# A decode step of two layers: W2 loaded twice, its buffer lent to a head's keys, the lead matrix dropped

## The chip, the cores and the metric

The kernel runs on one core of a Trainium2 chip. A core has a matrix engine (TensorE, PE in the profile; PEld is its weight load), a vector engine (VectorE, DVE), a scalar engine (ScalarE, ACT), GpSimd (POOL) and SyncE (SP, which here only issues transfers), and 16 transfer (DMA) engines that move data between the chip's main memory (HBM) and the on-chip buffer SBUF. Matrix products land in banks of a second small memory, PSUM. The metric is the device time of one execution in microseconds; lower is better.

## The reference

One token passes through attention with a cache, a dense block, and both once more with the same weights and the same cache. All data are float32.

```python
def _A_ref(x, k_cache, v_cache, wq, wo):            # H=32 heads, Sk=8192, Dh=128, D=640
    q = (x @ wq).reshape(1, 1, 32, 128).transpose(0, 2, 1, 3)
    scores = einsum("bhqd,bhkd->bhqk", q, k_cache) * 128 ** -0.5
    o = einsum("bhqk,bhkd->bhqd", softmax(scores), v_cache)
    return o.transpose(0, 2, 1, 3).reshape(1, 1, 4096) @ wo
def _B_ref(x, w1, w2):                              # Dff=1728
    return maximum(x @ w1, 0) @ w2
for _ in range(2):
    x = x + _A_ref(layernorm(x), k_cache, v_cache, wq, wo)
    x = x + _B_ref(layernorm(x), w1, w2)
```

Keys and values of a head are 4 MB each, so all 32 heads hold 268 MB. Both layers read all of them, and little of it fits on chip.

## The kernel before, in words

**The stream.** Keys and values come through one large buffer, `ring` (L94). Its room is counted in units of 8 numbers per partition, which over 128 partitions are 4 KB; `RING` is 3496. `UNITS` (L41 to L54) says in which pieces each head's cache is loaded: as a rule one load of all keys (1024 units, 4 MB) and one of all values; the heads at the ends of the layers are cut finer. `pump` (L123) issues, on SP's queue and in order, as many loads of the list `todo` as find room; `place` (L110) looks for the smallest free gap that holds the load in one piece. Each time PE has used a piece, `release` (L158) frees it and calls `pump` again. In SP's program the load stands behind a wait for the product that used the room last.

**Two layers, back and forth.** Layer 1 takes the heads 0 to 31, layer 2 the heads 31 to 0. What the ring holds at the end of layer 1 is not loaded again: head 31 whole and head 30 but for its first four units (`kept`, L96; together exactly `RING`). Those four (600 units) go to other buffers that are no longer needed then: `load_beside` (L143) loads them into `wqc`, `mix`, `lead` and `wct` as each is free. After that the ring takes head 29's keys when the first scores of layer 2 release room.

**One head.** `scores` (L361) multiplies the query with the keys, `exponentials` and `rows_weighed` do the softmax, `turn` transposes the weights, `values` (L420) multiplies with the values, `output` (L439) combines four rows. The heads' outputs are multiplied with `wo` in fours.

**The end of a layer.** The product of the last head's output with its `wo` rows and then W1 is not made one after the other: during the layer `mixing` and `mixing_quarter` (L474, L501) form the product of that part of `wo` with W1 in `mix`, so that `mlp` (L772) gets the hidden row from `o` with `mix` directly (L775). The hidden row is turned into columns `hT` (L822 to L859), passed through the ReLU, and multiplied with W2 in 14 blocks of 128 rows (`w2_t`, L877 to L901). Blocks 0 to 3 are summed on DVE into `by_rows` (L837, L887) and go through PE as one; the others go one by one.

**The start of layer 2.** The query of head 31, with which layer 2 begins, needs the layer norm of the whole output of layer 1. To have it sooner, layer 1 keeps the weights of that head's query in `wqc`, centred (`centred_weights`, L516), and forms the product of W2 with them in `lead` (`leading`, L532, one block in each of the heads 15 to 28) and that of the last head's output weights in `wct` (`leading_of_output`, L569). In `mlp` the query then follows from the hidden columns and `lead` (`lead_of`, L810), and the first scores of layer 2 begin while the output products of layer 1 still run (the `yield`s at L896 and L910). The scale from the layer norm follows later, in the exponentials (L380).

**Work beside the stream.** `due` (L669) puts side work in two lists; `work_off` does a step of it between the pieces of a head. W1, W2 and `wqc` are loaded on ACT's queue at the heads 4, 7 and 9 of layer 1 (L683 to L689), `wq` and `wo` in groups of four heads on the same queue.

Of the kernel before, what the change touches and what calls it, by code (L numbers as in the profile page):

```python
# [75 lines left out]
FB = 4 * F_TILES + F_REST  # L76


@with_exitstack
def decode_kernel(ctx: ExitStack, tc: tile.TileContext, x, kv, wq, wo, w1, w2, out):  # L80
# [41 lines left out]

    def pump():  # L123
        while todo:
# [3 lines left out]
            at = place(layer, n)  # L128
# [45 lines left out]
    def load_wq(g, queue):  # L174
        t = wts.tile([P, NB * HG * DH], F32, name="wq_t")
        n = NB * DH * (HG if g < NG - 1 else HG - 1)
        wq_t[g] = t[:, :n].rearrange("p (c n) -> p c n", c=NB)
        queue.dma_start(t[:, :n], wq[P * g : P * g + P, :n])
# [36 lines left out]


    wqc = consts.tile([P, NB, DH], F32, name="wqc")
    lead = consts.tile([P, FB, DH], F32, name="lead")

# [77 lines left out]
    second = []  # L297

    def weights_of(g, c, j):

        if g == NG - 1 and j == HG - 1:
            if not second:
                return wqc[:, c]
            j = 0
        return wq_t[g][:, c, j * DH : (j + 1) * DH]

    def queries(g, xc, r):

        pq = ps_m.tile([P, 512], F32, name="px")
        for c in range(NB):  # L310
            for j in range(HG):
# [3 lines left out]
                    weights_of(g, c, j),  # L315
# [200 lines left out]
    def centred_weights():  # L516
        pt = ps_m.tile([P, 512], F32, name="px")
        for c in range(NB):
            nc.tensor.matmul(
                pt[:, :DH],  # L520
                ones.to_broadcast([P, P]),
                wqc[:, c],
                start=(c == 0),
                stop=(c == NB - 1),
            )
        yield "dve"
        for c in range(NB):
            nc.vector.scalar_tensor_tensor(  # L528
                wqc[:, c], pt[:, :DH], -1.0 / D, wqc[:, c], op0=ALU.mult, op1=ALU.add
            )  # L530

    def leading(b):  # L532

        if b % 4 == 0:
            pt = ps_m.tile([P, 512], F32, name="px")
            n = min(4, FB - b)
            for i in range(n):
                for g in range(4):
                    nc.tensor.matmul(
                        pt[32 * g : 32 * g + 32, i * P : (i + 1) * P],  # L540
                        w2_t[:, b + i, g * DR + P : (g + 1) * DR],
                        ident,
                        start=True,
                        stop=True,
                    )
            yield "dve"
            nc.scalar.copy(lead[:, b : b + n].rearrange("p b d -> p (b d)"), pt[:, : n * P])
            yield "pe"
        pt = ps_m.tile([P, 512], F32, name="px")
        for c in range(4):  # L550
            nc.tensor.transpose(
                pt[:, c * P : (c + 1) * P], w2_t[:, b, c * DR : c * DR + P], ident
            )
        yield "dve"
        nc.scalar.copy(wct[:, :4].rearrange("p c d -> p (c d)"), pt)
        yield "pe"
        pt = ps_m.tile([P, 512], F32, name="px")
        for c in range(NB):
            nc.tensor.matmul(  # L559
                pt[:, :DH],  # L560
                wct[:, c] if c < 4 else lead[:, b],
                wqc[:, c],
                start=(c == 0),
                stop=(c == NB - 1),
            )
        yield "dve"
        nc.scalar.copy(lead[:, b], pt[:, :DH])

    def leading_of_output():  # L569

        pt = ps_m.tile([P, 512], F32, name="px")
        for c in range(NB):
            nc.tensor.matmul(
                pt[:, :DH], wct[:, c], wqc[:, c], start=(c == 0), stop=(c == NB - 1)
            )
        yield "dve"
        nc.scalar.copy(wct[:, 4], pt[:, :DH])

# [12 lines left out]
    def attention_and_mlp(L, xr, s, before=None):  # L591
# [44 lines left out]
        def before_last():  # L636
# [13 lines left out]
            if L == 0:  # L650
                pq = ps_m.tile([P, 512], F32, name="px")
                mlp_in.append(pq)
                for c in range(NB):
                    g = c % 4
                    nc.tensor.matmul(
                        pq[32 * g : 32 * g + 32, :DH],
                        xpc[:, c : c + 1].to_broadcast([P, 32]),
                        wqc[:, c],
                        start=c < 4,
                        stop=c in (2, 3, 4),  # L660
                        skip_group_check=True,
                    )
                load_beside(0, wqc.rearrange("p c d -> p (c d)"), NB * DH)
# [5 lines left out]
        def due(h):  # L669
# [20 lines left out]
            if L == 0 and where == MIX_AT[0][-1]:  # L690
                slow.append([centred_weights(), "pe"])
# [6 lines left out]
            if L == 0 and where == MIX_AT[L][-1] + 1:  # L698
                slow.append([leading_of_output(), "pe"])
            if where in LEAD_AT[L]:  # L700
                slow.append([leading(LEAD_AT[L].index(where)), "pe"])

# [69 lines left out]
    def mlp(L, o, last, xp, ph, pq=None):  # L772
# [7 lines left out]
        if L == 0:  # L780
            nc.tensor.matmul(
                pq[32:64, :DH],
                o.to_broadcast([P, 32]),
                wct[:, 4],
                start=False,
                stop=True,
                skip_group_check=True,
            )
        else:
            in_wait(64)  # L790
# [15 lines left out]
        if L == 0:  # L806
            nc.scalar.copy(xp[:, :DH], pq[:, :DH])
            pl = ps_m.tile([P, 512], F32, name="px")

        def lead_of(blocks):  # L810
            for b in blocks if L == 0 else ():
# [29 lines left out]
        if L:  # L841
            first_row()
# [164 lines left out]
```

## Time and profile before

| | us |
|---|---|
| median of 3 runs | 1367.67 (1367.07 to 1367.99) |
| the profiled execution, its own time | 1367.95 |
| its span, first to last instruction | 1366.1 |
| PE busy in it | 1000.2 (73%) |
| DVE, ACT busy | 182.7, 113.2 |

The profile divides the span into 40 slices of 34 us and gives for each the busy share of the engines in tenths, the granted PE clock, the share of the 16 DMA engines and what they moved. Further views list transfers by size, the chain of waits that ended last, the instructions in order of time, and busy times in chosen stretches. A tile is named without its buffer number; `w_t` stands for both W1 and W2, `in_kv` is the cache in HBM.

### The profile page before, as it was taken

To read this page: it belongs to the slowest core of one execution; us is meant where nothing else is said; L and a number is where in the kernel's file an instruction comes from. 1 tells how busy PE (TensorE), PEld (TensorE's weight loads), DVE (VectorE), ACT (ScalarE), POOL (GpSimd) and SP (SyncE) were. 2 spreads that over 40 slices of the span, in tenths; PEclk is the share of its full clock that TensorE was granted. 3 is DMA by queue.
4 is the path that set the end of the run, shared out by engine and by line. 5 is a ranking of instruction groups with operands and counts; after the bars stand their busy time and mean duration, and the time that the engine had idled before them with its cause. 6 is when DMAs were issued, how large, how long until landed. Compare 5 with 4: busy or idle time off the path is not lost.

```text
span 1366.1 us, 16729 instructions
## 1 busy us (share of the span) xinstructions
PE 1000.2 (73%) x7546; PEld 408.1 (30%) x7546; DVE 182.7 (13%) x696; ACT 113.2 (8%) x305; POOL 2.9 (0%) x10
## 2 busy tenths in 40 slices
PE   6674757778777777687798867677777677677768
PEld 2221312322333333333344322232223222222224
DVE  1010100111101111111122111110111111111112
ACT  0000000100101101111001000000001000000000
POOL 0000000000000000000000000000000000000000
PEclk8676777987888988987799777787779788887788
DMA  9999999999999999999979999999999999999994
GB/s 396 432 431 427 435 428 429 430 432 431 428 428 434 428 432 430 427 429 423 424 295 415 436 430 428 429 430 429 435 430 430 429 429 433 429 432 431 428 426 192
DMA packets 29023, 572.70 MB, mean 419 GB/s; under 512 B 3220, under 2 KB 3352, under 8 KB 5656
## 3 DMA queue, kind: packets, MB, share of 16 engines
q1 hardware_dynamic: 24056, 525.19, 89.9%
q10 hardware_dynamic: 4896, 46.45, 8.1%
q8 instruction: 59, 0.97, 0.3%
q14 instruction: 12, 0.10, 0.0%
HBM read 571.62 MB, written 0.00 MB: 418 GB/s over the span
## 4 chain that ended last, share of the span: by engine, by line
DMA 67%; PE 29%; DVE 2%; ACT 1%; issue 1%; SPq 0%; POOLq 0%; POOL 0%; ACTq 0%; DVEq 0%
DMA ring<-in_kv 65%; PE outs L427 10%; PE ps L366 10%; PE px L506 2%; PE pt L393 1%; DMA wo_t<-in_wo 1%; DMA wq_t<-in_wq 1%; PE px L312 1%; ACT p L385 1%; PE acc L332 1%; PE acc L582 1%; DVE h_t L378 1%; PE pm L413 1%; PE pm L453 0%; PE px L559 0%
## 5 line engine op out<-in xcount | busy, mean ns | idle before, releaser
L366 PE MATMUL ps<-ring,spread_q 128*32 128x512 f32 (+2 forms) x2064 | 315.9, 726 | 174.1 <-DMA ring<-in_kv 173.6
L427 PE MATMUL outs<-ring,pT 128*4 128x512 f32 (+2 forms) x2128 | 330.0, 770 | 57.1 <-DMA ring<-in_kv 56.9
L366 PEld LDWEIGHTS ps<-ring,spread_q 128*32 128x32 f32 x2064 | 61.0, 126 | 287.2 <-DMA ring<-in_kv 183.7
L427 PEld LDWEIGHTS outs<-ring,pT 128*4 128x4 f32 x2128 | 57.0, 101 | 264.2 <-issue 192.4
L378 DVE TENSOR_REDUCE h_t<-ps 128x1 f32<-128x512 f32 x64 | 44.2, 691 | 464.6 <-PE ps L366 464.4
L453 PE MATMUL pm<-h_t,p 128*128 128x1 f32 (+1 forms) x512 | 69.6, 258 | 33.1 <-DVE p L444 33.1
L453 PEld LDWEIGHTS pm<-h_t,p 128*128 128x128 f32 x512 | 64.4, 194 | 95.0 <-DVE p L444 93.4
L385 ACT ACTIVATE p<-ps,h_t 128x512 f32<-128x512 f32 x63 | 43.3, 687 | 556.9 <-DVE h_t L378 542.9
L393 PE MATMUL pt<-row_of,p 128*128 128x16 f32 x512 | 68.9, 267 | 22.8 <-ACT p L385 22.6
L444 DVE COPY p<-outs 128x256 f32<-128x256 f32 x62 | 26.3, 425 | 357.4 <-PE outs L427 357.4
L393 PEld LDWEIGHTS pt<-row_of,p 128*128 128x128 f32 x512 | 62.8, 193 | 34.6 <-ACT p L385 34.4
L445 ACT COPY p<-outs 128x256 f32<-128x256 f32 x62 | 23.1, 372 | 462.6 <-DVE p L444 462.6
L406 PE MATMUL pm<-ident,h_t 128*128 128x128 f32 x128 | 31.1, 325 | 40.2 <-DVE h_t L378 40.2
L506 PE MATMUL px<-w_t,wct 128*128 128x448 f32 (+1 forms) x80 | 46.7, 671 | 0.2 <-DVE wqc L528 0.2
L406 PEld LDWEIGHTS pm<-ident,h_t 128*128 128x128 f32 x128 | 19.0, 187 | 90.8 <-DVE h_t L378 88.7
L413 PE MATMUL pm<-h_t 128*128 128x1 f32 x128 | 26.9, 280 | 24.5 <-DVE h_t L410 24.5
L312 PE MATMUL px<-wq_t,ln_xc 128*32 128x128 f32 x630 | 30.8, 362 | 0.0
L312 PEld LDWEIGHTS px<-wq_t,ln_xc 128*32 128x32 f32 x630 | 26.3, 150 | 15.0 <-issue 14.0
L413 PEld LDWEIGHTS pm<-h_t 128*128 128x128 f32 x128 | 21.5, 210 | 30.8 <-DVE h_t L410 30.8
L332 PE MATMUL acc<-wo_t,o_cols 128*32 128x160 f32 x496 | 28.4, 384 | 0.0
L332 PEld LDWEIGHTS acc<-wo_t,o_cols 128*32 128x32 f32 x496 | 20.9, 145 | 19.4 <-issue 15.5
L506 PEld LDWEIGHTS px<-w_t,wct 128*128 128x128 f32 x80 | 13.7, 216 | 38.0 <-issue 36.9
(151 smaller groups left out, 343.2 us busy)
## 6 DMA issues: line engine op xcount, KB each, us to landing
ring<-in_kv SPq DMA_DIRECT2D x104, 4096.0 KB, 25.3
ring<-in_kv SPq DMA_DIRECT2D x27, 2048.0 KB, 23.8
ring<-in_kv SPq DMA_DIRECT2D x19, 1024.0 KB, 20.0
wo_t<-in_wo ACTq DMA_DIRECT2D x14, 1280.0 KB, 17.4
wq_t<-in_wq ACTq DMA_DIRECT2D x13, 1280.0 KB, 17.2
w_t<-in_w ACTq DMA_DIRECT2D x1, 4480.0 KB, 25.6
w_t<-in_w ACTq DMA_DIRECT2D x1, 4320.0 KB, 24.5
ring<-in_kv SPq DMA_DIRECT2D x3, 768.0 KB, 27.6
```

The costliest lines, as they stand in the source:

```text
L312: nc.tensor.matmul(pq[32 * j : 32 * j + 32, :DH], xc[:, c : c + 1].to_broadcast([P, 32]), weights_of(g, c, j), start=(c == 0), stop=(c == ...
L332: nc.tensor.matmul(acc[32 * g : 32 * g + 32, :DR], col.to_broadcast([col.shape[0], 32]), wt[:, g * DR : (g + 1) * DR], start=first, stop=last,
L366: nc.tensor.matmul(hd.ps[32 * g : 32 * g + 32, c : c + n], spread_q[:, 3 - r : 35 - r], tile_of[:, at + g * n : at + (g + 1) * n], start=f ...
L378: nc.vector.tensor_reduce(hd.nm, hd.ps, AX.X, ALU.max, negate=True)
L385: nc.scalar.activation(hd.p, hd.ps, AF.Exp, bias=hd.nm, scale=scale, accum_out=hd.l)
L393: nc.tensor.matmul(pt[:, 16 * b : 16 * b + 16], hd.p[:, b * P : (b + 1) * P], row_of.rearrange("p g r -> p (g r)"), start=True, stop=True,)
L406: nc.tensor.matmul(pt[:, :P], hd.nm.to_broadcast([P, P]), ident, start=True, stop=True)
L413: nc.tensor.matmul(pt[:, :1], hd.l.to_broadcast([P, P]), hd.wi, start=True, stop=True)
L427: nc.tensor.matmul((hd.out if r0 < 3 else hd.out_3)[32 * g : 32 * g + 4, r0:r1].rearrange("p r d -> p (r d)"), hd.pT[:, 4 * i : 4 * i + 4] ...
L444: nc.vector.tensor_copy(oc[:, :2], hd.out[:, :2])
L453: nc.tensor.matmul(pt[:, :n], oc[:, r], hd.w[:, r : r + 1].to_broadcast([P, n]), start=(r == 0), stop=(r == 3),)
L506: nc.tensor.matmul(pt[:, :n], wct[:, c], w1_t[:, c, f : f + n], start=(c == 0), stop=(c == NB - 1),)
```

## The change

- **W2.** Its load at head 7 of layer 1 is gone. `pump` now issues W2 in four parts (blocks 0 to 3, 4 to 7, 8 to 11, 12 and 13) on SP's queue, right behind the last load of layer 1 and again right behind the last one of layer 2.
- **Its buffer lent.** In the dense block of layer 1, behind the output products of blocks 3, 6, 9 and 12, the four key loads of head 29 are issued into `w2_t`, over blocks that are done. Head 29 is the third head of layer 2. Its keys thus no longer go through the ring there.
- **Lead matrix dropped.** `wqc`, `lead`, `centred_weights`, `leading`, `leading_of_output` and `lead_of` are gone. Layer 2's first query is now multiplied from the centred output of layer 1 with the weights in `wq_t`, after all output products. The last group of `wq` is loaded in one piece.
- **Ring.** `RING` becomes 3800. Kept are head 31 and head 30 but for two units (296 units); these two go to `mix` and `wct`. In layer 1, head 30's kept keys lie above 3072, all else below.
- **Order in the dense block.** In layer 1 all 14 blocks go through PE one by one, in order, after the spread of the rows; in layer 2 blocks 4 to 13 go in order, with `by_rows` at the end as before.

```diff
 UNITS[30] = [
+    ("k", [(0, 0, 432)]),
     ("k", [(0, 432, 80), (1, 0, 80)]),
-    ("k", [(0, 0, 432)]),
-    ("k", [(1, 80, 432), (2, 0, 16)]),
-    ("k", [(2, 16, 160)]),
-    ("k", [(2, 176, 336)] + K_ALL[3:]),
+    ("k", K_ALL[2:]),
+    ("k", [(1, 80, 432)]),
 ] + HALVES[2:]
...
-BESIDE = 4
-DROPPED = {30: BESIDE}
-RING = 3496
+DROPPED = {30: 2}
+BESIDE = DROPPED[30] + len(K_ALL)
+RING = 3800
...
-LEAD_AT = [range(15, 29), ()]
+FLAT = 3072
...
+W2_PARTS = [(0, 4), (4, 8), (8, 12), (12, FB)]
...
-    def place(layer, n):
+    def place(layer, u, n):
-        step = max(m for m in (8, 256, 512) if n % m == 0)
-        low, high = (0, RING) if layer else ((3072, RING) if n == RING - 3072 else (0, 3072))
+        step = max(m for m in (8, 64, 256, 512) if n % m == 0)
+        first_kept = u in kept and (u[0], UNITS[u[0]][u[1]][0]) == (30, "k")
+        low, high = (0, RING) if layer else ((FLAT, RING) if first_kept else (0, FLAT))
...
+            if not todo or layer < todo[0][0]:
+                for a, b in W2_PARTS:
+                    nc.sync.dma_start(w2_t[:, a:b], w2[:, a:b])
...
-            if L == 0 and where == 7:
-                nc.scalar.dma_start(w2_t, w2)
-            if L == 0 and where == 9:
-                n = NB * DH * (HG - 1)
-                nc.scalar.dma_start(wqc.rearrange("p c d -> p (c d)"), wq[P * (NG - 1) :, n:])
...
-            if where in LEAD_AT[L]:
-                slow.append([leading(LEAD_AT[L].index(where)), "pe"])
...
-            load_beside(1, mix, DFF)
+            load_beside(0, mix, DFF)
...
-            load_beside(3, wct.rearrange("p c d -> p (c d)"), NB * P)
-            r1 = spread_of_rows(ss)
-            lead_of(range(nb))
+            load_beside(1, wct.rearrange("p c d -> p (c d)"), NB * P)
...
+        ss = deviations(x1, s1)
         if L == 0:
...
+            r1 = spread_of_rows(ss)
+        for b in range(4 if L else 0, FB):
+            if L and b == 6:
                 for d in range(1, 4):
...
+            times_rows(po, w2_t[:rows, b], hT[:rows, b : b + 1], first, end)
+            if L == 0 and b in (3, 6, 9, 12):
+                i = b // 3 - 1
+                load_beside(DROPPED[30] + i, by_parts[:, 4 * RUN * i : 4 * RUN * (i + 1)], 4 * RUN)
+        if L:
+            times_rows(po, by_rows, ones, False, True)
...
         xc = at_once(centred(x2, s2))
+        pq = ps_m.tile([P, 512], F32, name="px")
+        for c in range(NB):
+            g = c % 4
+            nc.tensor.matmul(
+                pq[32 * g : 32 * g + 32, :DH],
+                xc[:, c : c + 1].to_broadcast([P, 32]),
+                wq_t[NG - 1][:, c, (HG - 1) * DH :],
+                start=c < 4,
+                stop=c in (1, 2, 3, 4),
+                skip_group_check=True,
+            )
+        row = work.tile([P, DR], F32, name="q_row")[:, :DH]
+        nc.vector.tensor_copy(row, pq[:, :DH])
+        pt = ps_m.tile([P, 512], F32, name="pm")
+        nc.tensor.matmul(pt[:, :1], row, one_of_each, start=True, stop=True)
+        spread_column(pt[:, :1])
         yield
         r = [spread_of_columns(xc)]
         yield r
-        second.append(1)
-        at_once(queries(NG - 1, xc, r))
+        for _ in queries(NG - 1, xc, r):
+            yield r
         yield x2, xc
```

More of the change, by code (lines that the diff above doesn't have):

```diff
@@ L127, in pump @@
             n = size(unit)
-            at = place(layer, n)
+            at = place(layer, u, n)
             if at is None:
@@ L295, in decode_kernel @@
     qT = {}
[L297 to L305, printed above, removed]
     def queries(g, xc, r):
@@ L514, in mixing_quarter @@
         nc.scalar.copy(mix[:, f : f + n], pt[:, :n])
[L516 to L577, printed above, removed]
     def hidden(ph, col, wt, first, last):
@@ L770, in attention_and_mlp, with mlp @@
         return mlp(L, o, last, *mlp_in)
-    def mlp(L, o, last, xp, ph, pq=None):
+    def mlp(L, o, last, xp, ph):
         hidden(ph, o, mix, False, True)
         if L == 0:
-            load_beside(1, mix, DFF)
+            load_beside(0, mix, DFF)
         pd = ps_m.tile([P, 512], F32, name="pm")
         times_rows(pd, wo_t[last // HG][:, last % HG], o, True, True)
[L780 to L790, printed above, removed]
+        in_wait(64)
         hr = wct.rearrange("p c d -> p (c d)")[:, : F_ROWS[0]]
@@ L805, in mlp @@
         )
[L806 to L811, printed above, removed]
-                g, rows = b % 4, 2 * half if b == nb + 1 else P
-                nc.tensor.matmul(
-                    pl[32 * g : 32 * g + 32, :DH],
-                    hT[:rows, b : b + 1].to_broadcast([rows, 32]),
-                    lead[:rows, b],
-                    start=b < 4,
-                    stop=b >= FB - 4,
-                    skip_group_check=True,
-                )
         for j in range(F_TILES):
@@ L829, in mlp @@
             )
-            if j == 0 and L == 0:
-                ss = deviations(x1, s1)
-                in_wait(192, "acc")
-        by_rows = work.tile([P, D], F32, name="p")
-        def first_row():
+        if L:
+            by_rows = work.tile([P, D], F32, name="p")
             nc.vector.tensor_scalar(
```

61 lines of the change are left out of this document (9 added, 52 removed).

## The prediction

> **What bounds the kernel now.** I read the page first: busy shares, the slices, the chain by engine.
>
> ```profile
> span 1366.1 us, 16729 instructions
> ...
> DMA  9999999999999999999979999999999999999994
> GB/s 396 432 431 427 435 428 429 430 432 431 428 428 434 428 432 430 427 429 423 424 295 415 436 430 428 429 430 429 435 430 430 429 429 433 429 432 431 428 426 192
> DMA packets 29023, 572.70 MB, mean 419 GB/s; under 512 B 3220, under 2 KB 3352, under 8 KB 5656
> ...
> DMA 67%; PE 29%; DVE 2%; ACT 1%; issue 1%; SPq 0%; POOLq 0%; POOL 0%; ACTq 0%; DVEq 0%
> ```
>
> The kernel is a stream of transfers. Only two slices of 34 us sag: number 21, where layer 1 turns into layer 2, and the last. So a time is: bytes at full rate, plus what the stream idles at these places. Next come windows. Columns: stretch, length, then busy time of PE, PEld, DVE, ACT, POOL, then PE clock, DMA share, GB/s.
>
> ```profile
> 40.00:680.00 640.00, 461.23 (x3404) 191.18 (x3404) 76.58 (x284) 59.23 (x158) 0.00 (x0) 0.81 1.00 429
> 760.00:1332.00 572.00, 414.20 (x2868) 156.52 (x2860) 71.02 (x264) 43.00 (x117) 0.00 (x0) 0.80 1.00 430
> 698.00:704.00 6.00, 5.62 (x80) 3.22 (x76) 1.04 (x5) 1.07 (x3) 0.00 (x0) 1.00 0.51 204
> 704.00:710.00 6.00, 5.68 (x65) 3.84 (x56) 2.60 (x13) 0.56 (x3) 0.00 (x0) 1.00 0.20 44
> 710.00:716.00 6.00, 5.85 (x102) 3.30 (x104) 3.82 (x11) 0.00 (x0) 0.55 (x1) 1.00 0.97 329
> 716.00:722.00 6.00, 5.85 (x114) 3.67 (x106) 2.29 (x12) 0.00 (x0) 0.55 (x1) 1.00 0.94 341
> 1332.00:1344.00 12.00, 10.41 (x76) 4.47 (x80) 1.30 (x6) 0.37 (x1) 0.00 (x0) 0.72 0.99 420
> 1344.00:1352.00 8.00, 7.62 (x92) 4.23 (x88) 1.73 (x6) 1.07 (x3) 0.00 (x0) 1.00 0.45 185
> 1352.00:1366.00 14.00, 10.48 (x166) 6.86 (x158) 6.41 (x22) 0.37 (x2) 0.55 (x1) 0.94 0.01 1
> ```
>
> Full rate is 429.5 GB/s, the mean of the first two rows. Against it each later row lost its length times (1 - rate/429.5). The layer change: 3.15 + 5.39 + 1.40 + 1.24 = 11.2 us. The tail: 4.55 + 13.97 = 18.5 us. In the change's first 6 us the share is 0.51: part of the transfer engines finish the last values some 6 us ahead of the others.
>
> **The change part by part.**
>
> *Bytes.* Sizes come from the table of issues (KB is 1024 bytes; last column, us to landing).
>
> ```profile
> ring<-in_kv SPq DMA_DIRECT2D x19, 1024.0 KB, 20.0
> ...
> wq_t<-in_wq ACTq DMA_DIRECT2D x13, 1280.0 KB, 17.2
> w_t<-in_w ACTq DMA_DIRECT2D x1, 4480.0 KB, 25.6
> ...
> mix<-in_kv SPq DMA_DIRECT2D x1, 864.0 KB, 4.5
> ...
> wct<-in_kv SPq DMA_DIRECT2D x1, 320.0 KB, 3.1
> ```
>
> W2's 4480 KB travel once more: 10.68 us at full rate. The ring keeps 304 more units of 4 KB (3800 against 3496; a 256-unit load is the 1024 KB row), so layer 2 loads 1216 KB less: 2.90 us. The last head's query weights travel as before, in one load and not two. Net +3264 KB, **+7.78 us** if nothing hides it.
>
> *Layer 1 without W2.* The stream reaches the last values 10.68 us sooner. The preparation of the lead matrix (PE, ACT, DVE work in heads 13 to 28) and two issues on ACT's queue disappear: costed at nothing, since the row of 40 to 680 shows the stream full over them and PE with 179 us free.
>
> *The layer change.* Timeline of before (start, us, engine, line, operation):
>
> ```profile
> 693.08 0.51 PE L655 MATMUL px<-wqc,ln_xc 128*32 128x128 f32 x9 [0.51 <-DVE ln_xc L259]
> ...
> 704.34 0.34 PEld L427 LDWEIGHTS outs<-ring,pT 128*4 128x4 f32 x8 [0.30 <-DMA ring<-in_kv]
> ...
> 707.96 0.33 SPq L147 DMA_DIRECT2D mix<-in_kv  x1
> ...
> 709.94 0.23 PE L853 MATMUL acc<-sel,wct 128*32 128x1 f32 x4
> ...
> 711.96 0.35 DVE L873 SCALAR_TENSOR_TENSOR xr<-px,ln_r,xr 128x128 f32<-128x128 f32 x1 [1.16 <-PE px L813]
> ...
> 713.02 1.06 PE L366 MATMUL ps<-ring,spread_q 128*32 128x512 f32 x8
> ...
> 716.12 1.27 PE L332 MATMUL pt<-w_t,hT 128*32 128x160 f32 x32
> ...
> 717.73 0.38 DVE L905 SCALAR_TENSOR_TENSOR xr<-pt,ln_r,xr 128x160 f32<-128x160 f32 x1 [1.55 <-PE pt L332]
> ...
> 719.54 0.23 DVE L259 TENSOR_SCALAR ln_xc<-pm,ln_m 128x5 f32<-128x5 f32 x1
> ```
>
> Call 704.34, when the last values are there, t0. Layer 2's first scores follow at t0+8.7. In the changed kernel the hidden rows are ready as now at t0+5.8 (709.94+0.23). The spread of the rows, now interleaved, follows (two products and three DVE steps, about 1.4 us by rows of this size): output products from t0+7.2. Fourteen blocks at 1.27/4 = 0.32 take 4.5: t0+11.7. W2's parts end 3.05, 6.1, 9.15 and 10.7 us behind the values, so they are there in time. From x2 to its centred columns 2.04 us (717.73 to 719.77): t0+13.7. The query without the lead matrix takes one more set of products (0.5, by 693.08) and then what 711.96 to 713.02 holds, 1.1: first scores at t0+15.4. **PE's path grows by 6.7 us, but t0 comes 10.7 us sooner**: scores at 709.1 instead of 713.0.
>
> What must decide is whether the stream has work meanwhile. Before, it had 600 units. Now it has W2 (10.68 us), the mix and wct loads (864 and 320 KB, 2.8 us, issued about t0+3.6 and t0+5.9), and four keys of head 29 (9.76 us). The first of these is behind output block 3, t0+8.5, and wct's 3.1 us for 0.76 us of bytes says that an issue into an empty queue costs 2.3 more. Engines that are early wait some 2 us, late ones nothing: about 1 us. On SP's queue the four W2 loads stand behind the last values, the key loads wait for PE, and behind them stand only ring loads, which wait for the first scores anyway (t0+16.5). The keys last until about t0+20. No hole there.
>
> The next doubtful place is further on. Rows of the chain and of ACT's issues:
>
> ```profile
> 724.83 3.55 PE outs L427 x40
> ...
> 751.68 6.10 PE outs L427 x32
> 757.79 17.26 DMA ring<-in_kv
> ```
> ```profile
> 722.20 0.33 ACTq L178 DMA_DIRECT2D wq_t<-in_wq  x1
> ...
> 743.62 0.34 ACTq L178 DMA_DIRECT2D wq_t<-in_wq  x1
> ```
>
> Head 27's keys need 1024 units in one piece. By the placement rule they get them at the end of head 29's values (757.79 now), and after the change when half of these are used: 754.7 on today's clock. PE loses the products interleaved with the scores (two runs of 1.27), so 724.83 turns into 709.1 + 11.8 - 2.6 = 718.3, 6.5 sooner, and the issue comes at 748.2, its bytes about 750.5. The stream runs from 701.2 - 10.68 = 690.5 (t0 less the 3.15 lost ahead of it) through 4480 + 864 + 320 + 4096 + 4096 + 8192 + 2x1280 = 24608 KB, 58.7 us: until 749.2. [...]
>
> So the idle at the change goes from 11.2 to **3 us**. Bounds: 1 (the early engines' wait alone) and 8 (what is lost today behind t0, the rows of 704 to 722). I take 3: 1 + 1.3 + 0.7 for the clock, nearer the low end since the queue can be followed load by load.
>
> *The tail.*
>
> ```profile
> 1358.17 0.54 DVE L837 TENSOR_SCALAR p<-w_t,hT 128x640 f32<-128x640 f32 x1
> ...
> 1358.67 2.65 PE L332 MATMUL px<-w_t,hT 128*32 128x160 f32 x64
> ...
> 1362.33 0.48 PE L332 MATMUL px<-p,ones 128*32 128x160 f32 x8
> ...
> 1362.49 0.55 POOL L232 TENSOR_TENSOR ln_r<-ln_v,mhalf 128x1 f32<-128x1 f32 x1 [640.98 <-DVE ln_v L230]
> ...
> 1363.07 0.38 DVE L905 SCALAR_TENSOR_TENSOR xr<-px,ln_r,xr 128x160 f32<-128x160 f32 x1 [0.73 <-POOL ln_r L232]
> ```
>
> The second W2 load fits into 18.5 idle us. The last values land by 1352 at the slowest engines and at 1347.5 in the mean, W2 thus at 1358.1 (mean) to 1362.7. PE wants blocks 0 to 3 at 1358.17 (they land by 1355 even late), and reaches blocks 12 and 13 at 1361.3. At worst two blocks and the last product follow 1362.7: 1363.8, against 1363.04 where POOL now releases the end. Cost of the tail +0.5 us; bounds -1 (PE's clock was 0.72 from 1332 to 1344; it need not be) and +2.
>
> *Sum.* 1366.1 + 7.78 - (11.2 - 3) - (10.68 - 0.5) = 1355.5 span; the profiled execution took 1.85 more (1367.95), so 1357.3, and that execution lies 0.28 above the median 1367.67: **1357.0 us**, 0.8% faster.
>
> [...] A stretch of layer 1 that is all loads of 1024 KB:
>
> ```profile
> 645.00:661.00 16.00, 13.87 (x84) 5.17 (x84) 2.39 (x9) 1.45 (x4) 0.00 (x0) 0.71 1.02 423
> ```
>
> Short loads in a full queue lose 1.5%, so cutting W2 in four costs nothing in my sum. [...]
>
> **The rivals.**
>
> *PE is late after the change* (slower clock, a longer path than t0+15.4). Each us beyond it leaves the stream dry before head 27's keys. For: PE is busy 5.6 to 5.9 of each 6 us from 698 to 722 at a clock of 1.00, which is 0.81 in the mean of layer 1. At the upper bound 8: 1362; a further us: 1363.
>
> *W2 lands late at the end.* If the engines drift further apart than 4.5 us, its last part holds the end: +2 to +4: 1359 to 1361.
>
> *The loads mix (slower side).* W2's four loads are issued while the last values are still under way. If the engines served them together, the values would land up to 10.7 us late, at both layer ends. t0 is then 704.3 again, scores at 719.7, and head 27's keys are issued at 748.2 + 10.7 = 758.9; with 2.3, their 9.8 and some 2.5 of drift they land at 773.5 against 775.05 now (757.79 + 17.26). That is 1.5 us gained, and at the end 10.7 less about 1.5 of slack lost: 1375. It turns slower from about 6 us of such delay. Against it: all ring loads go through SP's queue, and the short last ones (1024 KB, 20.0 us to landing, no less than what is queued ahead) do not overtake. [...]
>
> *Each transfer pays 2.3 us* (the wct row): three more, +7: 1364. The row of 645 speaks against it.
>
> **How the numbers follow.** Forecast (1353 to 1360, idle at the change 1 to 6 and the tail's bounds) 0.74; PE late 0.11; W2 late 0.06; loads mix 0.06; fixed cost 0.03. The range **1353 to 1363** takes in the first three, 0.91, of which I leave some 0.08 for what passes the bounds. What differs by less than 0.2% (2.7 us) can't be told from no change. Faster 0.88, same 0.04, slower 0.08; the last from the mixing case and what I have missed.
>
> **What would show it.** Right: bytes 576.0 MB; no slice under 400 GB/s at the layer change; the last values of layer 1 about 10.7 us sooner; first scores of layer 2 about 15.4 us behind them; last slice still low. Wrong: PE waiting for W2 at the output products, the last values later than 694, a hole before head 27's keys of over 4 us, or a stretch of layer 2 under 425 GB/s.

## The result and the profile after

The changed kernel takes 1363.76 us (median of 5, 1359.98 to 1365.76) against 1367.99 us (5 runs, 1367.07 to 1368.81): ratio 0.9967, interval 0.9955 to 0.9978. The interval leaves out 1, so it is faster, but by 4.2 us where 10.7 were forecast, and it lies 0.76 us above the upper end of the range. Its profiled execution took 1363.76 us, its span is 1361.9 us; the sum in the prediction had 1355.5 us for the span. 6.4 us are missing.

The page of the changed kernel, the same lines as of the kernel before:

```profile
span 1361.9 us, 15957 instructions
...
PEclk9677688788887777787788877778778877787878
DMA  9999999999999999999999999999999999999997
GB/s 393 432 433 431 428 431 431 430 429 429 432 430 432 429 432 431 427 426 425 426 377 406 393 440 426 431 428 430 434 427 430 430 432 429 432 428 433 431 424 302
DMA packets 29452, 576.00 MB, mean 423 GB/s; under 512 B 3268, under 2 KB 3400, under 8 KB 5320
```

The bytes are those of the prediction (576.0 MB). The last slice rises from 192 to 302 GB/s, slice 21 from 295 to 377; but the two slices behind it fall from 415 and 436 to 406 and 393, and the prediction had no slice under 400 at the layer change. The windows of the changed kernel (columns as in the prediction) show where:

```profile
688.00:694.00 6.00, 5.62 (x80) 3.18 (x76) 1.04 (x5) 1.07 (x3) 0.00 (x0) 1.00 1.02 424
694.00:700.00 6.00, 5.69 (x66) 3.80 (x56) 2.26 (x11) 0.37 (x2) 0.00 (x0) 0.99 0.91 359
700.00:706.00 6.00, 5.04 (x71) 3.83 (x75) 0.98 (x6) 0.00 (x0) 0.55 (x1) 0.50 0.80 296
706.00:712.00 6.00, 4.42 (x76) 2.97 (x68) 1.07 (x5) 0.00 (x0) 0.00 (x0) 0.78 0.99 362
712.00:718.00 6.00, 5.74 (x64) 2.64 (x67) 0.40 (x4) 0.00 (x0) 0.55 (x1) 0.59 0.99 403
718.00:724.00 6.00, 4.31 (x38) 2.24 (x34) 2.16 (x10) 1.08 (x3) 0.00 (x0) 0.98 0.98 340
...
754.00:766.00 12.00, 9.86 (x80) 4.23 (x76) 2.10 (x8) 1.45 (x4) 0.00 (x0) 0.93 0.89 358
766.00:1334.00 568.00, 420.12 (x2896) 159.01 (x2888) 70.84 (x265) 42.33 (x115) 0.00 (x0) 0.78 1.00 430
1334.00:1348.00 14.00, 13.02 (x154) 6.68 (x150) 2.72 (x10) 1.07 (x3) 0.00 (x0) 1.00 1.00 416
1348.00:1356.00 8.00, 5.54 (x86) 4.26 (x82) 4.97 (x16) 0.37 (x2) 0.00 (x0) 0.74 0.57 234
1356.00:1362.00 6.00, 2.70 (x30) 1.10 (x26) 0.55 (x3) 0.00 (x0) 0.55 (x1) 0.50 0.00 0
```

The column that was 1.00 in every row of the layer change before, PE's clock, is now 0.50 from 700 to 706 and 0.59 from 712 to 718. Loss is again length times (1 - rate/429.5). One row takes in the whole layer change; in the changed kernel it is

```profile
694.00:766.00 72.00, 61.78 (x614) 31.25 (x608) 14.32 (x64) 5.79 (x17) 1.10 (x2) 0.83 0.95 382
```

8.0 us of idle stream, where the prediction took 3. From 1334 to the end the rows lose 0.44 + 3.64 + 5.9 = 10.0 us. Before, the rows from 1332 lost 0.27 + 4.55 + 13.97 = 18.8, so the prediction's saving of 10.2 would have left 8.6. So 5.0 us of the 6.4 are missing at the layer change and 1.4 at the end.

The timeline of the changed kernel, at the layer change and at the end:

```profile
701.59 6.63 PE L321 MATMUL px<-w_t,hT 128*32 128x160 f32 x112
...
712.56 1.94 PE L355 MATMUL ps<-ring,spread_q 128*32 128x512 f32 x8 [0.27 <-DVE spread_q L343]
...
755.13 0.33 SPq L134 DMA_DIRECT2D ring<-in_kv  x1
...
1346.90 0.94 PE L508 MATMUL acc<-mix,c_ol 128*32 128x448 f32 x8 [0.25 <-DVE c_ol L449]
...
1350.68 1.30 PE L321 MATMUL px<-w_t,hT 128*32 128x160 f32 x32 [0.63 <-DVE q_row L277]
1353.75 2.36 PE L321 MATMUL px<-w_t,hT 128*32 128x160 f32 x32 [1.76 <-DVE p L745]
```

Layer 1's output products take 6.63 us and not 4.5, the first score products 1.94 and not 1.06; the first scores start at 712.56 and not at 709.1. Head 27's keys are issued at 755.13 and not at 748.2, so 3.5 us are added ahead of the first scores and another 3.5 behind them. From the first scores to the point where half of head 29's values are used, PE had a clock of 0.90 before and has 0.83 now:

```profile
713.02:754.70 41.68, 37.55 (x442) 18.79 (x442) 11.73 (x42) 4.05 (x11) 0.55 (x1) 0.90 1.00 405
```
```profile
712.56:755.13 42.57, 37.60 (x342) 16.46 (x346) 7.70 (x34) 3.97 (x11) 0.55 (x1) 0.83 0.97 398
```

At the end PE waits 1.76 us between blocks 7 and 8, and then needs 2.36 us for what took 1.30 just before. The wait is put down to DVE's sum over rows, on which these products do not depend; what they need is W2's third part. A second profile of the same kernel names it:

```profile
1350.97 2.36 PE L321 MATMUL px<-w_t,hT 128*32 128x160 f32 x32 [1.79 <-DMA w_t<-in_w]
```

Theory A: PE's clock falls during the layer change, since the change put short products that wait for DVE in the place of longer ones; PE's path from the last values to layer 2's first scores grows, and with it the moments at which PE releases room. Theory B: the engines that are early, the order of issues or the room for head 27's keys cost the time, whatever the clock. Theory W: at the end W2 comes too late.

### The profile page after: what moved, and what is told of

It is laid out like the page before. It is cut to its first block, busy times and chain, and to the rows that moved or that the text cites. A ratio compares the mean times of both kernels' runs of the same rounds, so it can differ in the third digit from the quotient of the medians.

```text
span 1361.9 us, 15957 instructions
## 1 busy us (share of the span) xinstructions
PE 987.3 (72%) x7180; PEld 388.5 (29%) x7180; DVE 178.7 (13%) x687; ACT 99.5 (7%) x271; POOL 2.9 (0%) x10
## 4 chain that ended last, share of the span: by engine, by line
DMA 67%; PE 30%; DVE 2%; ACT 1%; issue 1%; SPq 0%; ACTq 0%; DVEq 0%
DMA ring<-in_kv 66%; PE outs L416 10%; PE ps L355 10%; PE px L495 2%; PE pt L382 1%; PE px L301 1%; PE acc L321 1%; DMA wo_t<-in_wo 1%; ACT p L374 1%; PE px L321 1%; DVE h_t L367 1%; PE acc L508 1%; PE pm L402 1%; PE pm L442 1%; DVE pT L390 0%
## 5 line engine op out<-in xcount | busy, mean ns | idle before, releaser
L355 PE MATMUL ps<-ring,spread_q 128*32 128x512 f32 (+1 forms) x2024 | 321.3, 759 | 177.4 <-DMA ring<-in_kv 176.6
L416 PE MATMUL outs<-ring,pT 128*4 128x512 f32 (+2 forms) x2128 | 333.9, 780 | 53.4 <-DMA ring<-in_kv 53.3
L355 PEld LDWEIGHTS ps<-ring,spread_q 128*32 128x32 f32 x2024 | 65.8, 132 | 312.3 <-DMA ring<-in_kv 187.8
L321 PE MATMUL acc<-wo_t,o_cols 128*32 128x160 f32 x496 | 32.1, 421 | 0.0
L321 PEld LDWEIGHTS acc<-wo_t,o_cols 128*32 128x32 f32 x496 | 22.6, 155 | 19.9 <-issue 15.9
```

The costliest lines, as they stand in the source:

```text
L321: nc.tensor.matmul(acc[32 * g : 32 * g + 32, :DR], col.to_broadcast([col.shape[0], 32]), wt[:, g * DR : (g + 1) * DR], start=first, stop=last,
L355: nc.tensor.matmul(hd.ps[32 * g : 32 * g + 32, c : c + n], spread_q[:, 3 - r : 35 - r], tile_of[:, at + g * n : at + (g + 1) * n], start=f ...
L416: nc.tensor.matmul((hd.out if r0 < 3 else hd.out_3)[32 * g : 32 * g + 4, r0:r1].rearrange("p r d -> p (r d)"), hd.pT[:, 4 * i : 4 * i + 4] ...
```

## The experiments

Ratios are to the kernel before, run beside each on the same chip. The runs below come from four chips; only the ratio is carried from one to the next.

**Fillers in PE's waits.** A filler (`in_wait`) is a product whose result nobody reads; the number is its columns.

```diff
+            if j == 0 and L == 0:
+                in_wait(192, "acc")
...
         if L == 0:
+            in_wait(384)
             r1 = spread_of_rows(ss)
...
+        in_wait(192)
         xc = at_once(centred(x2, s2))
+        in_wait(192)
...
+        in_wait(128)
         pt = ps_m.tile([P, 512], F32, name="pm")
         nc.tensor.matmul(pt[:, :1], row, one_of_each, start=True, stop=True)
         spread_column(pt[:, :1])
+        in_wait(64)
```

> Edit: in layer 1's dense block, products whose result nobody reads are put into PE's waits (192 columns behind the first hidden columns, 384 ahead of the spread of the rows, 192 twice around the centring of the output, 128 and 64 around the first query). Theory A, the clock: in the changed kernel PE's granted clock is 0.50 from 700 to 706 and 0.53 to 0.50 from 710 to 716, where the kernel before had 1.00; the path to layer 2's first scores is thereby some 3.5 us longer than I summed, and the stream idles for it. Then the clock stays at 1.00 over the output products, these take 4.6 us and not 6.6, the first scores come about 3 us sooner, and the time falls from 1363.8 to about 1360.5. Rival B, the engines that are early and the order of the issues cost it, not the clock: within 1 us of 1363.8, or up to 2 us slower since the products take time themselves.

Measured: 1358.45 us, ratio 0.9928 (0.9915 to 0.9941). Windows and timeline of this kernel:

```profile
694.00:766.00 72.00, 63.65 (x640) 31.01 (x636) 15.01 (x66) 6.11 (x18) 1.11 (x2) 0.91 1.00 414
700.00:706.00 6.00, 5.68 (x119) 4.13 (x118) 0.98 (x6) 0.00 (x0) 0.56 (x1) 1.00 0.90 340
706.00:712.00 6.00, 5.92 (x84) 3.67 (x87) 1.08 (x7) 0.00 (x0) 0.55 (x1) 1.00 1.01 419
...
1327.20:1333.20 6.00, 5.40 (x36) 2.43 (x36) 0.38 (x2) 0.00 (x0) 0.00 (x0) 0.52 0.97 409
```

```profile
700.83 4.39 PE L321 MATMUL px<-w_t,hT 128*32 128x160 f32 x112
...
708.85 1.06 PE L355 MATMUL ps<-ring,spread_q 128*32 128x512 f32 x8
...
1349.10 1.29 PE L321 MATMUL px<-w_t,hT 128*32 128x160 f32 x32 [0.18 <-DMA w_t<-in_w]
```

The clock is 1.00 over the whole path, the output products take 4.39 us, the first scores start at 708.85 (forecast for the changed kernel: 709.1), the layer change loses 2.6 us (forecast 3), and the span is 1355.2 us (forecast 1355.5). With the clock that the sum had assumed, the path and the sum come out, as theory A has it. Part of the match of the span is luck: this execution is the fastest of five (1357.06; the median is 1.4 us above the forecast 1357.0), and its loss at the change falls elsewhere than forecast (below). The size of the gain, 3.3 us expected and 5.3 by medians, is taken over two chips here; it was measured again on one chip, below.

**The second load of W2 left out.**

```diff
-            if not todo or layer < todo[0][0]:
+            if todo and layer < todo[0][0]:
```

> Edit: the second load of W2, behind the last values of layer 2, is left out, so that layer 2's output products multiply with what is left in the buffer. Theory: W2 lands too late there, PE waits 1.8 us between blocks 7 and 8 and then runs at half clock; without the load the end is as in the kernel before, 7.9 us from the product with mix to the last sum and not 12.3: about 4.4 us off, 1359.4. Rival: the wait is for DVE's sum over rows or the clock alone, and the load is hidden as I forecast: 1363 to 1363.8.

Measured: 1360.39 us (1356.81 to 1362.86), 0.9938 (0.9922 to 0.9955). The interval overlaps that of the changed kernel's first measurement by a little, and the kernel's two later measurements (0.9947 and 0.9958, below) lie closer still, so the gain of 3.4 us in time is not shown. What the timeline does show is that there is no wait between the blocks of the output products, and that from the product with `mix` to the end of the last sum it takes 7.9 us as in the kernel before, where the changed kernel takes 12.3:

```profile
1349.78 0.94 PE L508 MATMUL acc<-mix,c_ol 128*32 128x448 f32 x8 [0.25 <-DVE c_ol L449]
...
1352.86 2.38 PE L321 MATMUL px<-w_t,hT 128*32 128x160 f32 x64
```

**Head 27 in halves.**

```diff
+UNITS[27] = HALVES
```

> Edit: head 27's keys and values are loaded in halves of 512 units, so that its first half finds room when head 30's values are used, not head 29's. Theory: the changed kernel loses 2.5 us between 742 and 766 because the load of 1024 units is issued only at 755; with halves this loss goes to under 0.5 and the time falls by 2 us to about 1361.8. Rival: the stream is short there because PE is late with releasing room in all, and the loss moves to the next loads: no change, 1363 to 1364.

Measured: 1360.94 us, 0.9945 (0.9933 to 0.9957). The loss between 742 and 766 goes from 2.5 to 0.05 us; 724 to 742 loses 1.0 where it lost 0.15. So the missing room in one piece is real, and part of the loss moves. By time the gain is not clear of the changed kernel's later measurements. Nor is the path the same: in this profile PE's clock was 1.00 from 700 to 706 without any filler. Whether halves help once PE is in time, the run with fillers and halves below tells.

**W2 loaded once, nothing lent.** The second load is left out as above, and

```diff
-BESIDE = DROPPED[30] + len(K_ALL)
+BESIDE = DROPPED[30]
...
-            if L == 0 and b in (3, 6, 9, 12):
-                i = b // 3 - 1
-                load_beside(DROPPED[30] + i, by_parts[:, 4 * RUN * i : 4 * RUN * (i + 1)], 4 * RUN)
```

> Edit: W2 is loaded once, behind layer 1's last values, and stays; head 29's keys go through the ring in layer 2 as in the kernel before. Against the changed kernel the stream carries 4.59 MB less (10.7 us), but has nothing to do between the small loads at the layer change and the first scores (about 10 us idle there, against 8.0 in all now, and the slow start of 2 to 3 us behind it), and the end is idle as before. By my accounting 1365 to 1368: the lending is worth 2 to 4 us. Rival, that the lending gains nothing and only costs its bytes: 1357 to 1360.

Measured: 1364.96 us (1362.53 to 1371.48), 0.998 (0.9968 to 0.9993). The stream stands still where the key loads of head 29 would be:

```profile
706.00:712.00 6.00, 4.15 (x56) 2.42 (x52) 1.31 (x8) 0.00 (x0) 0.00 (x0) 0.77 0.02 9
```

Against the changed kernel's first measurement (0.9967, 0.9955 to 0.9978) no difference is shown; against the second (0.9947, 0.9934 to 0.9961, on another chip) the intervals do not meet. So the lending pays for its bytes; what it gains beyond them as the kernel stands, between nothing and some 4 us, is not resolved.

**The changed kernel again, and one filler alone.** The first is the changed kernel unaltered; the second has of the fillers only the one that the change took away (192 columns behind the first hidden columns).

> The changed kernel as it is, on the chip of the next three, for the comparison. Both theories: 1362 to 1365, ratio to the kernel before 0.996 to 0.998. If the clock falls at another moment in each execution, its times spread over some 4 us.

> Edit: of the fillers only the one that the change dropped comes back (192 columns behind the first hidden columns). Theory A1, the dropped filler alone lets the clock fall: as with all fillers, 5 us faster than the changed kernel. Theory A2, it is the new chain of short products (spread ahead of the output products, centring, query, each waiting for DVE): 0 to 2 us faster, the clock still falls between 700 and 716.

Measured: 1361.43 us, 0.9947 (0.9934 to 0.9961), and 1361.84 us, 0.9946 (0.9934 to 0.9958). No difference is shown in time. The changed kernel came out lower than the 0.996 to 0.998 expected. The profile with one filler fits neither A1 nor A2, whose sign was a clock that still falls between 700 and 716: here it was 1.00 from 694 to 718. The stream lost 9.3 us all the same, since the last head's output came 3 us late (699.79) and PE was slow again behind the first scores (the table below). So the lost filler is not shown to be the cause, and neither is the new chain of waits by this run.

**Fillers and halves; and a filler at the end.** Both on the chip of the two above. The last adds

```diff
+            if L and b == 8:
+                in_wait(512)
```

> Edit: all fillers and head 27 in halves. If the hole before head 27's keys comes from PE being late and has gone with the clock (0.3 us are left between 742 and 766 with the fillers), the halves add nothing: within 0.7 us of the fillers alone. If it is the missing room in itself, 1 to 2 us faster than the fillers alone.

> Edit: as the one before, and in layer 2's dense block a product of 512 columns that nobody reads, where PE waits for W2's third part. If half clock after that wait costs at the end (56 instructions at 0.50 in the changed kernel's profile, some 2 us), the time falls by up to 2 us; if W2 arrives in time since PE is late anyway, the product's own 1.1 us is added: 0 to 1 us slower.

Measured: 1359.53 us, 0.9932 (0.9921 to 0.9944), and 1358.58 us, 0.9924 (0.9912 to 0.9936). With fillers the halves add nothing that shows. Fillers do not always hold the clock: in the first of these two profiles it was 0.72 from 700 to 706 and the output products took 5.82 us. The filler at the end is worth 1 us by the medians; the intervals overlap.

**The path made longer.** To the fillers four more are added ahead of the first query.

```diff
+        for _ in range(4):
+            in_wait(512)
```

> Edit: all fillers, and four more products of 512 columns that nobody reads ahead of the first query (4.3 us by 1.06 for such a piece). Theory A: the path from the last values to layer 2's first scores sets what the stream idles from there to head 27's keys; some 1.5 us of cover are left, so 2.5 to 4 us slower than the fillers alone (1358.5 becomes 1361 to 1362.5). Rival: the length of this path does not matter and the fillers help elsewhere: within 1 us of the fillers alone.

Measured: 1362.97 us, 0.9957 (0.9941 to 0.9973): 4 us more than the fillers alone by ratio (0.9928, 0.9915 to 0.9941; the intervals touch). Windows and timeline:

```profile
694.00:766.00 72.00, 64.85 (x598) 31.78 (x598) 13.32 (x59) 5.00 (x15) 1.10 (x2) 0.86 0.91 371
...
712.00:718.00 6.00, 5.98 (x76) 3.29 (x80) 0.69 (x5) 0.00 (x0) 0.55 (x1) 1.00 0.73 280
```

```profile
700.69 5.82 PE L321 MATMUL px<-w_t,hT 128*32 128x160 f32 x112
...
714.73 1.06 PE L355 MATMUL ps<-ring,spread_q 128*32 128x512 f32 x8
```

The first scores start 5.9 us later than in the profile of the fillers alone: 4.3 are the added products, 1.4 the output products, which took 5.82 us and not 4.39 in this execution. The layer change loses 9.8 us instead of 2.6; 2.1 of it from 712 to 718, where PE is busy 5.98 of 6 us at a clock of 1.00. So a longer path costs the stream by itself, at a full clock too, and the clock can act through it.

**The kernel before without its filler.**

```diff
-                in_wait(192, "acc")
```

> Edit, in the kernel before: its one filler in layer 1's dense block (192 columns) is taken out. If this filler keeps the clock up there: 1 to 3 us slower than the kernel before, with a clock under 1.00 between 704 and 716. If the clock there hangs on the lead matrix's products and the rest, as the single filler in the changed kernel let one think: within 1 us.

Measured: 1368.18 us, 0.9999 (0.9987 to 1.0011). No difference is shown there either.

**Fillers, and no second load of W2.**

> Edit: all fillers, and the second load of W2 left out, so that layer 2's output products multiply with what is left in the buffer. Theory: at the end PE waits 0.2 to 1.8 us for W2's third part and then runs on at half clock; without the load 1 to 3 us faster than the fillers alone. Rival: the load is hidden once PE's clock is right: within 0.7 us.

Measured: 1356.78 us, 0.9916 (0.9899 to 0.9933). The medians say 1.7 us, the intervals overlap: W2's price at the end, with fillers, is not resolved.

**The spread of the rows later.**

```diff
-        if L == 0:
-            r1 = spread_of_rows(ss)
...
-            if L and b == nb:
+            if b == (nb if L else 6):
                 r1 = spread_of_rows(ss)
```

> Edit: the fillers, and the spread of layer 1's rows moved from ahead of the output products to behind the sixth of them (a filler of 64 columns instead of 384 there). PE then does not wait about 1 us for DVE ahead of the products: by theory A the first scores come 0.7 to 1 us sooner and the key loads of head 29 too; 0.5 to 1 us faster than the fillers alone, since the early engines wait less. Rival: within 0.3 us, the path has cover by now.

Measured: 1359.43 us, 0.9935 (0.9918 to 0.9951): no gain shows. The path from the last head's output to the first scores is 12.3 us and not 13.0, the 0.7 us expected, but in this execution that output came 1.0 us later (696.83 against 695.83), so the first scores came at 709.09, no sooner than 708.85.

**Which waits, on one chip.** The changed kernel a third time, the fillers ahead of the output products alone, those behind them alone, and all.

> The changed kernel on the chip of the next three. By both theories a ratio to the kernel before of 0.995 to 0.997.

> Edit: only the fillers ahead of the output products (192 behind the first hidden columns, 384 ahead of the spread). If the wait of 1 us for DVE ahead of the products lets the clock fall at 700, as the changed kernel's first profile suggests, this brings most of the gain: 2 to 3 us faster than the changed kernel. If the waits behind the products count, under 1 us.

> Edit: only the fillers behind the output products (192 twice around the centring, 128 and 64 around the first query). If these waits let the clock fall at 710, 2 to 3 us faster than the changed kernel; if the wait ahead of the products counts, under 1 us.

> All fillers, on the same chip as the changed kernel. Theory A: 3 to 5 us faster than the changed kernel, with intervals of the ratios that do not overlap. Rival: the gap was one between chips, under 2 us.

| kernel | median us | ratio (interval) |
|---|---|---|
| changed | 1363.54 | 0.9958 (0.9942 to 0.9974) |
| fillers ahead of the products | 1361.36 | 0.9946 (0.9933 to 0.9958) |
| fillers behind them | 1359.82 | 0.9935 (0.9922 to 0.9947) |
| all | 1358.27 | 0.9921 (0.9909 to 0.9934) |

All fillers against none: 5.3 us, and the intervals do not meet. The two halves bring 2.2 and 3.7 us by medians, each not clear of its neighbour. The rows of the layer change, one per fence, of the changed kernel here and of the kernel with all fillers:

```profile
694.00:766.00 72.00, 62.76 (x648) 31.04 (x640) 13.55 (x60) 4.71 (x14) 1.10 (x2) 0.83 0.91 360
```

```profile
694.00:766.00 72.00, 63.69 (x650) 31.22 (x643) 15.04 (x66) 5.98 (x18) 1.10 (x2) 0.91 1.00 415
```

11.7 us are lost in the one and 2.4 in the other. Not all of this is the fillers' work: in the first of the two profiles the last head's output comes 3.3 us later, ahead of every filler, and PE loses another 3.6 us behind the last of them (below). The changed kernel with all fillers beats both the changed kernel and the kernel before.

**What sets the idle time at the change.** The prediction has the stream's work last until 749.2 and its bytes flow again 2.3 us behind the issue of head 27's keys. Its own sum, with the moment at which these keys were really issued, can be set against the loss from 694 to 766 in each profile that has head 27's keys in one load and head 29's keys lent. Columns: start of the last head's output (row of `c_ol`), from there to the first scores, from these to the issue (in brackets PE's clock over this stretch), the issue, issue + 2.3 - 749.2, and the measured loss; all in us.

| profile | output | to scores | to issue (clock) | issue | sum | loss |
|---|---|---|---|---|---|---|
| forecast | 696.0 | 13.1 | 39.1 | 748.2 | 1.3 | 3 |
| changed, first | 696.7 | 15.9 | 42.6 (0.83) | 755.1 | 8.2 | 8.0 |
| changed, second | 696.0 | 14.1 | 42.3 (0.84) | 752.4 | 5.5 | 5.6 |
| changed, third | 699.7 | 16.0 | 42.9 (0.82) | 758.6 | 11.7 | 11.7 |
| second load of W2 left out | 695.3 | 13.4 | 45.2 (0.76) | 753.8 | 6.9 | 6.8 |
| one filler | 699.8 | 12.8 | 43.5 (0.79) | 756.2 | 9.3 | 9.3 |
| fillers ahead of the products | 696.6 | 13.0 | 45.2 (0.76) | 754.7 | 7.8 | 8.0 |
| fillers behind them | 696.0 | 13.1 | 42.2 (0.82) | 751.2 | 4.3 | 4.4 |
| all fillers, first | 695.8 | 13.0 | 40.7 (0.87) | 749.6 | 2.7 | 2.6 |
| all fillers, on the last chip | 696.4 | 12.8 | 39.2 (0.90) | 748.4 | 1.5 | 2.4 |
| all fillers, no second load of W2 | 696.6 | 12.8 | 42.2 (0.82) | 751.6 | 4.7 | 4.4 |
| all fillers, spread later | 696.8 | 12.3 | 42.0 (0.84) | 751.1 | 4.2 | 4.1 |
| path made longer | 695.7 | 19.0 | 42.2 (0.82) | 756.9 | 10.0 | 9.8 |

In all twelve the wait of SP for the issue ends with PE's products of head 29's values. In eleven the sum gives the loss to 0.3 us; in the twelfth the keys are issued so early that what is lost ahead of them, 2.5 us up to 742, is all there is. So the idle time is set by one moment: when PE has used half of head 29's values. PE can be late there by the last head's output, by the path to the first scores, or by its pace behind them, and that last stretch is mostly the longer the lower its clock (39.2 us at 0.90, 45.2 at 0.76). That stretch holds no filler, and its clock is 0.87 and 0.90 in two profiles with all fillers and 0.82 in a third. On the path itself the fillers bring 1 to 3 us; where the rest of the 5.3 us by medians comes from is not shown.

## Why the prediction was wrong

- **The step that failed: PE's times at the change, "first scores at t0+15.4" and from there "the issue comes at 748.2".** Every term of the path to the first scores (4.5 us for fourteen blocks, 2.04 us for the centring, 0.5 and 1.1 us for the query) came from rows at a clock of 1.00, and the new path was taken to run at it too. In the first profile PE ran at 0.50 over most of the products: 6.63 us for the blocks, first scores at 712.56 instead of 709.1. Behind them PE was taken at the pace of the kernel before (clock 0.90), and ran at 0.83: another 3.5 us. Head 27's keys were issued at 755.13, 6.9 us late, and the stream idled for 8.0 us instead of 3. With all fillers and a clock of 1.00 the same path gave 708.85.
- **"I take 3 us" for the idle at the change.** It was 8.0, the upper bound given. Of the 3 us 0.7 stood for a slower clock, and only for head 27's keys. No run shows that 0.7; in its place the first profile has a clock of 0.83 from the first scores to the issue, where the kernel before had 0.90, and 42.6 us for this stretch, where the forecast had 39.1. The other terms, "1 + 1.3" (1.3 is 750.5 - 749.2), count the early engines' wait twice: an idle 1 us ahead of 749.2 lets the work last 1 us longer, and the hole before head 27's keys shrinks by it. That 2.3 is close to the 2.6 and 2.4 us measured with all fillers is luck. There 2.2 and 2.5 us are lost up to 742, where 1 was forecast, and 0.4 and nothing in the hole, where 1.3 was.
- **The hole before head 27's keys** was found at the right place, and its cause is the one named: PE is late at the middle of head 29's values. In the first profile 2.5 us are lost there, and 5.5 before it, which the prediction put at 1. With all fillers the hole is 0.4 us and nothing in two profiles, 1.9 in a third.
- **"the queue can be followed load by load"** as the reason for the low end. The queue could; what sets the times of its issues, PE's clock, could not, and that should have widened the bound, not narrowed it. The rival "PE is late after the change" was the right mechanism, priced at 1362 to 1363 with a chance of 0.11.
- **The tail, +0.5 us.** It cost 1.9. That is within its bounds. PE came to the third part of W2 before it was there: 1.76 us of waiting, then a clock of 0.50 (1353.75 to 1356.10). The sum set PE's times from the kernel before, where PE itself was late at the end (clock 0.72 from 1332 to 1344), and so found W2 in time; in the changed kernel the clock was 1.00 from 1334 to 1348. In the first profile with all fillers it was 0.52 from 1327 to 1333, and PE waited 0.18 us for W2. With fillers and halves it was 1.00 there, the wait was 1.79 us and the span 1360.1 us, though the layer change lost only 3.3. So the tail too hangs on PE's clock, and the span of the first profile with fillers met the sum to 0.3 us partly because PE was late at the end as before.
- **Right:** the bytes; the values of layer 1 sooner by W2's transfer (706.69 for the last head's output becomes 696.71, 10.0 us); W2 in time for the output products of layer 1 (they run through without a wait in the first profile, and wait under 0.3 us for one part in a few others); no mixing of W2's loads with the last values (with the mixing that the rival priced, these 10.0 us would be gone); the loads cut in parts without a cost of their own that shows: with all fillers the medians are 1358.45 and 1358.27 against 1357.0 forecast.

What stays open is why the clock falls at a given moment. It falls at other times in other executions of the same kernel: in the three profiles of the changed kernel it was 0.50, 0.72 and 0.79 from 700 to 706, and 0.78, 0.91 and 0.64 from 706 to 712. Three profiles of the changed kernel and two with all fillers, from the last head's output (row of `c_ol`) to the first scores:

```profile
696.71 0.16 DVE L449 COPY c_ol<-pm 128x1 f32<-128x1 f32 x1 [1.10 <-PE pm L442]
```
```profile
695.98 0.16 DVE L449 COPY c_ol<-pm 128x1 f32<-128x1 f32 x1 [1.10 <-PE pm L442]
...
710.12 1.14 PE L355 MATMUL ps<-ring,spread_q 128*32 128x512 f32 x8 [0.27 <-DVE spread_q L343]
```
```profile
699.74 0.16 DVE L449 COPY c_ol<-pm 128x1 f32<-128x1 f32 x1 [1.10 <-PE pm L442]
...
715.71 1.94 PE L355 MATMUL ps<-ring,spread_q 128*32 128x512 f32 x8 [0.27 <-DVE spread_q L343]
```
```profile
695.83 0.16 DVE L449 COPY c_ol<-pm 128x1 f32<-128x1 f32 x1 [1.10 <-PE pm L442]
```
```profile
696.43 0.16 DVE L449 COPY c_ol<-pm 128x1 f32<-128x1 f32 x1 [1.10 <-PE pm L442]
...
709.21 1.06 PE L355 MATMUL ps<-ring,spread_q 128*32 128x512 f32 x8
```

That is 15.9, 14.1 and 16.0 us without fillers and 13.0 and 12.8 with them; the prediction's own working gives 709.1 - 696.0 = 13.1. In the third profile the last head's output is itself 3 us late, so PE is late there before this path begins. The paths with and without fillers overlap: without, 13.4 us with the second load of W2 left out and with head 27 in halves; with all fillers and halves, 14.4. Of the seven profiles with all fillers five have a clock of 1.00 over the output products and two have not (5.82 us for the blocks in both), of the six with none two have and four have not (5.80 to 6.91 us). So the fillers do not secure the clock; that they make it fall less often is likely from so few, not shown. That the spread of the changed kernel's times, 1359.98 to 1365.76, comes from this is likely, not shown.

## What to carry to other kernels

A path priced from rows has the clock of those rows in it, and so has PE's pace in every later stretch that sets an issue. Where an edit replaces long products by a chain of short ones that wait for another engine, price the path at the lowest clock that the profile shows as well, and let the range reach there (here the fourteen blocks took 4.39 us at a clock of 1.00 and 6.63 with 0.50 over most of them). In a kernel that streams, find the one load whose issue waits for PE and follow PE up to it: here the idle time was that issue, less the moment at which the queued work ended, and stops ahead of it were not added to it but taken up in it. 4.3 us of added work cost about 4 us here.

## What had not been expected of the hardware

PE's clock fell from 0.98 to 0.50 although PE was busy by the profile. The stretch ahead of the fall in the changed kernel's first profile and the one behind it, and the same two with all fillers:

```profile
696.60:700.00 3.40, 3.09 (x35) 2.14 (x34) 1.50 (x9) 0.37 (x2) 0.00 (x0) 0.98 0.84 321
700.00:703.40 3.40, 2.44 (x31) 1.91 (x35) 0.98 (x6) 0.00 (x0) 0.55 (x1) 0.50 0.89 355
```
```profile
696.60:700.00 3.40, 3.34 (x36) 2.42 (x26) 1.74 (x10) 0.37 (x2) 0.00 (x0) 1.00 0.93 359
700.00:703.40 3.40, 3.20 (x79) 2.78 (x82) 0.58 (x4) 0.00 (x0) 0.56 (x1) 1.00 0.88 325
```

PE is busy 91% of the one stretch and 98% of the other, and the clock behind them is 0.50 and 1.00. The busy share is not what tells them apart: where the second load of W2 was left out, with no filler, PE is busy 70% of the same stretch of time and the clock stays at 1.00.

```profile
696.60:700.00 3.40, 2.38 (x28) 2.05 (x28) 2.09 (x12) 0.37 (x2) 0.00 (x0) 1.00 0.99 385
700.00:703.40 3.40, 3.26 (x92) 2.82 (x96) 0.16 (x1) 0.00 (x0) 0.56 (x1) 1.00 0.87 317
```

None of the stretches shown is idle, and no run here took apart what decides which of them is followed by a clock of 0.50.
